# A fused linear-attention and SwiGLU kernel: the last group's outputs over three queues, and one more Strassen pair in group 3

## The chip, the cores and the metric

The kernel runs on one core of a Trainium2 chip. The time is the device time of one execution in microseconds (us); three runs before the change gave 297.36, 297.43 and 297.45, so the median is 297.43. The profile is of one further execution, whose own time was 297.82 us.

## The reference

The inputs are q, k and v with 8 batches, 8 heads, 576 positions and 64 channels, and three weight matrices. What is computed, cut to its core:

```python
q_p, k_p = phi(q), phi(k)                       # phi(x) = elu(x) + 1
kv = einsum('bhsd,bhse->bhde', k_p, v)
num = einsum('bhsd,bhde->bhse', q_p, kv)
den = einsum('bhsd,bhd->bhs', q_p, sum(k_p, axis=2))[..., None] + 1e-06
x = (num / den).transpose(0, 2, 1, 3).reshape(4608, 512)
g, val = x @ w_gate, x @ w_val                  # 512 -> 1536
out = (g * sigmoid(g) * val) @ w_out            # 1536 -> 512, float32
```

## The kernel before

The 4608 tokens are cut into 72 units of 64 (9 per batch), and 8 units make one of 9 groups of 512 tokens. For each group TensorE makes the normalized attention output (`x_prd`), then layer 1 (gate and value), then layer 2 (`l2_prd`), and the results go from SBUF to DRAM. The attention of later batches is prepared between: `phis` (feature map of k and q), `kv_prd` (the 64x64 state of a batch), `chain` and `norm` (denominator, reciprocal, and the scaling of q, `s3_scale`), and `tr`, a transposing DMA on SyncE's queue that turns scaled q for `x_prd`.

**Layer 1.** A column block of 128 hidden features costs 16 matmuls of 512 columns for two blocks of the plain form (`c_chunk`, L826: two matmuls an operation). A *pair* of blocks can be made in Strassen's form instead (`pair_prd`, L351: seven products of four matmuls with 256 columns). A pair needs more work on the other engines: five ScalarE copies or silus (L365, L368) and four VectorE operations (L371 twice, L855, L864), where the two plain blocks need two silus and two multiplications (L374). `NP` says how many of a group's six pairs are made so: 3 in groups 2 and 3, 5 in groups 4 and 5, 6 from group 6 on. With fewer than four pairs, `layer_1` alternates pair products and plain chunks; with four or more it runs the pair products staggered and puts the plain chunks at the end, and fills the first slots with what the group before left over (`tail`).

**Layer 2** is Strassen's form throughout (`prd`, L456): seven products numbered 1 to 7, each for two token tiles `tt` 0 and 1, of six matmuls with 256 columns. The string `ORDER[g]` gives their order: `60` is product 6 of tile 0; a letter after it takes part of its six matmuls (`a`: the first four, `c` the fifth, `d` the sixth, `e` the first five). `M` is the next group's `x_prd`, `J` a `kv_prd`; what stands behind `|` is left to the next group's layer 1. Sums of the hidden tile, `hs` (`h_sum`, L425), feed products 3, 5, 6, 7. A product is taken out of PSUM by `keep` (ScalarE, L465, to a partial sum), `fin` (VectorE, L470, product plus partial sum to the output tile `osb`) or `copy_half` (ScalarE, L461).

**Order.** Every operation of groups 1 to 8 is put on a list with the tiles it reads and writes, and a list of 1362 numbers, `steps`, gives the order in which they are issued. Each engine works strictly in that order.

**Output of the last group (8).** Each quarter of an output tile (128 partitions by 256 columns) goes out in two transfers of 64 rows by 1 KB, `put_1` (L1014), issued by `out_op`. Of 16 transfers, 13 are issued on SyncE's queue (SP), two on ScalarE's and one on GpSimd's (POOL).

**Scaling of q.** `S3[b]`/`SCALE[b]` give the position chunks of batch b that are summed and scaled one group before their batch is first used; `S3L[b]`/`SCALEL[b]` those left to the next group. Batch 4 is done whole: summed as (0,5),(5,9), scaled in threes. Batch 5 is split: (0,5) early, (5,9) late.

`WL` says before which group the weight sums for Strassen's products (`wl_sum`) of the second half of the hidden features are put on the list.

Of the kernel before, what the change touches and what calls it, by code (L numbers as in the profile page):

```python
# [10 lines left out]
ALU = mybir.AluOpType  # L11
AX = mybir.AxisListType

P = 128
# [3 lines left out]
def kernel(  # L18
# [420 lines left out]
    def prd(g, n, tt, fs, seeded):  # L439
# [15 lines left out]
        for (i, f) in enumerate(fs):  # L455
            nc.tensor.matmul(out=(z if n in (2, 3, 5) else x)[:, 0:HD], lhsT=left(f), rhs=right(f),  # L456
                             start=(i == 0 and fs[0] == 0 and (n in (1, 5) or n == 2 and not seeded)),
                             stop=(i == len(fs) - 1), skip_group_check=True)
# [9 lines left out]
    def fin(tt, th, ch, i, from_x):  # L468
        (x, z) = l2_banks(tt)
        nc.vector.scalar_tensor_tensor(out=osb[2 * th + tt][:, HD * ch:HD * ch + HD],  # L470
                                       in0=(x if from_x else z)[:, 0:HD], scalar=1.0 / SC, in1=part[:, 2 * i + tt, :],
                                       op0=ALU.mult, op1=ALU.add)
# [333 lines left out]
    def nm(t):  # L806
        return bank[id(t)]
# [10 lines left out]
    NP = {1: 0, 2: 3, 3: 3, 4: 5, 5: 5, 6: 6, 7: 6, 8: 6}  # L818
# [103 lines left out]
    KVB = {**{b: ["X2", "V2"] for b in range(B)}, 2: ["X0", "X1"], 7: ["X1", "V0"], 6: ["X1", "V0"], 5: ["X1", "V0"]}  # L922
# [34 lines left out]
    def l2_prd(g, n, tt, fs=tuple(range(HF)), done=True):  # L957
# [11 lines left out]
        if n == 1:  # L969
            if sd:  # L970
                op("ACT", 0.3, lambda: copy_half(x, seed_bank(tt)[:, 0:HD], 1.0), [nm(x)], [nm(seed_bank(tt))])
            else:
                op("ACT", 0.3, lambda: keep(tt, 0, True), [nm(x)], [f"part0{tt}"])
        if n == 2:
            if sd:
                op("ACT", 0.3, lambda: copy_half(dst, o1[:, 0:HD], 1.0 / SC), [nm(dst)], [f"o{tt}.0"])
            else:
                op("DVE", 0.34, lambda: fin(tt, 0, 0, 0, False), [nm(z), f"part0{tt}"], [f"o{tt}.0"])
# [6 lines left out]
        if n == 7:  # L985
            op("DVE", 0.34, lambda: fin(tt, 1, 1, 2, True), [nm(x), f"part2{tt}"], [f"o{2 + tt}.1"])
            if last:
                out_op(g, tt, 1, 1, (nc.sync, nc.scalar) if tt else (nc.sync, nc.sync))
        if n == 3:
            op("DVE", 0.34, lambda: fin(tt, 0, 1, 1, False), [nm(z), f"part1{tt}"], [f"o{tt}.1"])  # L990
            if last:
                out_op(g, tt, 0, 1, (nc.sync, nc.gpsimd) if tt else (nc.sync, nc.sync))
            else:
                op("SP", 0.12, lambda: put(g, tt, 0), [f"o{tt}.0", f"o{tt}.1"], [])
        if n == 4:
            if last and tt:
                op("DVE", 0.34, lambda: nc.vector.tensor_scalar(out=o2[:, 0:HD], in0=x[:, 0:HD], scalar1=1.0 / SC, scalar2=None,
                                                                op0=ALU.mult), [nm(x)], [f"o{2 + tt}.0"])
                out_op(g, tt, 1, 0, (nc.sync, nc.scalar))
# [7 lines left out]
    def out_op(g, tt, th, ch, engs=(nc.sync, nc.sync)):  # L1007
        for e in range(2):
            eng = {id(nc.sync): "SP", id(nc.scalar): "ACT", id(nc.gpsimd): "POOL"}[id(engs[e])]
            op(eng, 0.06, lambda e=e: put_1(g, tt, th, ch, e, engs[e]), [f"o{2 * th + tt}.{ch}"], [])  # L1010
# [78 lines left out]
    WL = {2: [(1, 1, 1), (2, 0, 1)], 3: [(2, 1, 1), (3, 0, 1)], 4: [(3, 1, 1)]}  # L1089
# [45 lines left out]
    ORDER[99] = ""; S3[7], SCALE[7], S3L[7], SCALEL[7] = ((0, 1),), ((0, 1),), ((1, 5), (5, 9)), ((1, 3), (3, 6), (6, 9)); S3[6], SCALE[6], S3L[6], SCALEL[6] = ((0, 2),), ((0, 2),), ((2, 5), (5, 9)), ((2, 5), (5, 9),); S3[5], SCALE[5], S3L[5], SCALEL[5] = ((0, 5),), ((0, 3), (3, 5)), ((5, 9),), ((5, 9),)  # L1135

    ORDER.update({g: "10 11 20 21 60 61 50 51 70 71 M 30 31 | 41 40 J" for g in (3,4)})

    def program():
# [21 lines left out]
        0 1 4 14 15 9 17 18 10 5 20 21 23 6 24 26 27 16 29 3 19 30 32 8 2 33 35 36 7 22 38 28 41 25 39 40 42 31  # L1161
        34 44 45 43 37 47 63 46 48 64 49 105 66 12 50 67 69 106 65 70 51 11 72 68 73 52 75 71 13 76 114 78 77 79
        74 81 80 82 84 53 83 85 54 87 86 88 90 55 89 91 107 93 56 94 92 96 95 57 97 99 98 100 58 102 59 101 103
        113 127 104 60 129 108 128 109 131 117 171 133 110 132 130 135 112 115 137 134 139 111 136 125 138 120
        141 116 143 119 142 145 140 118 122 147 146 144 150 124 126 148 153 121 162 151 156 61 165 155 154 123
        168 62 149 152 163 167 158 176 164 157 172 177 169 159 179 166 170 178 160 181 161 197 180 342 199 182
        200 343 183 198 202 184 204 201 206 203 174 207 185 209 208 205 211 186 210 214 215 173 212 218 220 219
        213 222 175 221 187 223 225 216 224 227 217 229 228 188 230 285 226 232 231 189 234 236 235 237 233 240
        242 238 241 245 243 246 239 248 190 247 250 244 249 252 251 253 276 255 191 254 257 256 259 277 192 258
        193 260 262 261 264 194 267 265 268 263 271 266 273 269 272 274 270 284 298 275 300 278 280 299 302 279  # L1170
        301 286 281 304 303 282 306 288 308 305 287 310 307 296 309 289 312 283 314 313 311 316 290 291 318 317
        315 293 321 319 324 322 297 292 333 326 336 294 325 334 195 339 327 328 347 329 196 320 348 504 323 340
        335 338 350 330 341 337 349 331 352 368 332 353 370 354 369 371 355 373 372 375 356 295 377 357 378 380
        379 376 382 381 358 385 386 351 383 389 344 387 391 393 390 392 394 374 384 396 359 398 397 388 400 360
        399 401 395 403 456 405 402 404 407 345 408 406 411 409 413 346 412 361 416 410 414 417 419 415 418 421
        364 423 422 424 420 426 425 362 428 430 429 447 431 363 365 448 427 433 432 435 438 436 439 434 442 437
        444 440 443 445 441 455 469 446 471 449 470 450 473 457 451 475 452 474 472 477 459 476 479 453 478 481
        467 480 454 462 483 458 485 484 460 487 482 464 486 489 488 498 461 491 501 490 366 468 492 505 499 493
        367 507 494 500 506 496 510 508 495 512 466 502 463 515 503 509 517 497 513 465 516 523 514 518 525 519
        511 527 529 524 528 540 526 542 541 545 543 531 547 546 629 550 530 552 548 551 554 532 553 556 544 558  # L1180
        555 561 557 559 563 562 549 566 560 564 568 567 570 565 569 533 572 571 574 573 577 620 579 575 578 582
        580 576 584 534 586 583 588 585 587 590 589 593 581 591 595 594 598 621 521 600 596 602 601 603 599 535
        606 592 604 608 607 611 597 605 612 609 520 614 613 615 536 617 616 522 618 628 610 642 537 619 644 622
        643 624 646 632 623 648 625 626 645 650 635 647 652 649 627 654 651 653 637 656 633 658 634 657 660 655
        700 630 662 661 671 659 663 640 631 674 664 672 641 666 667 677 665 675 679 636 678 682 668 680 684 639
        669 670 687 638 689 688 701 694 538 685 691 696 690 702 683 539 698 673 676 681 686 706 695 703 715 697
        699 717 716 704 720 707 722 721 725 718 708 705 727 726 723 729 728 731 709 719 733 730 736 732 734 738
        737 724 741 739 743 742 745 710 804 744 747 735 749 746 752 748 750 754 753 740 757 755 751 759 758 761
        711 756 763 760 762 765 764 768 712 770 766 769 773 713 693 775 771 777 714 778 767 776 781 774 779 783
        782 772 786 780 784 787 692 789 797 788 790 792 798 791 793 785 803 815 795 794 817 796 816 819 799 807  # L1190
        800 821 820 801 818 823 805 825 822 802 827 824 826 810 829 808 831 871 830 806 833 828 812 832 835 834
        844 872 836 809 847 837 845 838 873 850 846 839 852 840 848 851 855 841 849 853 842 857 814 843 854 860
        874 862 811 861 865 858 875 864 867 813 859 863 856 869 876 882 866 891 870 868 893 892 877 896 894 884
        898 897 901 880 883 903 902 905 895 899 907 904 909 906 908 900 912 910 914 913 917 885 911 915 919 918
        921 886 916 923 920 887 922 925 924 928 878 930 929 933 926 879 881 935 934 931 937 936 888 939 927 938
        941 944 940 889 932 946 890 945 942 949 951 947 950 953 979 952 955 954 943 957 960 980 956 962 948 961
        958 965 968 963 959 969 966 971 972 970 967 974 964 973 975 977 978 981 976 989 990 991 992 993 983 996
        982 998 1000 997 1002 984 1004 999 985 1011 994 1003 1006 1001 1013 988 995 1015 987 1014 1007 1017 1012
        1016 986 1005 1019 1047 1018 1021 1008 1020 1023 1009 1022 1026 1024 1028 1010 1027 1025 1048 1031 1029
        1033 1049 1032 1030 1036 1034 1050 1038 1037 1035 1051 1041 1039 1052 1043 1042 1040 1045 1053 1044 1060  # L1200
# [46 lines left out]
```

## Time and profile before

| | us |
|---|---|
| median of three runs | 297.43 |
| profiled execution, its own time | 297.82 |
| its span, first to last instruction | 296.0 |
| PE busy | 286.4 (97%) |
| weight load (PEld) busy | 212.9 (72%) |
| VectorE (DVE) busy | 258.6 (87%) |
| ScalarE (ACT) busy | 236.3 (80%) |
| GpSimd (POOL) busy | 42.5 (14%) |

Two kinds of view are used. A *timeline* has, for each piece of an engine's work, start and length in us, engine, line, operation, destination and source, and the number of instructions merged into it. A *windows* row has the length of a stretch and then the busy time of PE, PEld, DVE, ACT and POOL, each with its number of instructions, the granted share of TensorE's clock (1.00 nearly everywhere here), the DMA engines' mean busy share and GB/s. Issues of transfers on SP's and ACT's queues appear as SPq and ACTq.

### The profile page before, as it was taken

Reading aid. Unit: us, or ns where it says so; the run is one execution under the profiler, and the core shown is the slowest. Engines: PE = TensorE matmul, PEld = TensorE weight load, DVE = VectorE, ACT = ScalarE, POOL = GpSimd, SP = SyncE. Lnnn points to the kernel's source line nnn. Section 1 sums busy time; section 2 is a strip of 40 time slices with the busy share of each in tenths; the row PEclk is TensorE's granted clock in tenths of the full one; section 3 lists DMA queues with packets and bytes.
Section 4 is the critical chain, followed back from the end, with each engine's and each line's share of the span. In section 5 each row is a group of like instructions: output and inputs, shape, how many; then the busy total and the mean of one; then the engine's idle time right before and its main releaser. Section 6 shows DMA issues by size and latency. Waiting matters only on the chain.

```text
span 296.0 us, 7377 instructions
## 1 busy us (share of the span) xinstructions
PE 286.4 (97%) x2939; PEld 212.9 (72%) x2939; DVE 258.6 (87%) x521; ACT 236.3 (80%) x405; POOL 42.5 (14%) x55
## 2 busy tenths in 40 slices
PE   7899999999999999999999999999999999999991
PEld 5644454454866687668887888788888888788881
DVE  4667889999999998999899999999999999757961
ACT  4773977983998689969999999999986688668830
POOL 8554436500000011000100010000000000000000
PEclk9999999999999999999999999999999999999999
DMA  7999999995598319661960669304140443050014
GB/s 203 193 196 200 205 207 207 196 216 87 81 171 190 64 15 171 162 105 33 147 181 2 105 98 222 61 2 100 44 73 2 99 95 22 2 129 15 0 41 103
DMA packets 41506, 32.92 MB, mean 111 GB/s; under 512 B 16432, under 2 KB 36848, under 8 KB 41472
## 3 DMA queue, kind: packets, MB, share of 16 engines
q0 software_dynamic: 20176, 18.35, 40.7%
q1 hardware_dynamic: 21136, 13.97, 21.0%
q8 instruction: 23, 0.38, 0.5%
q10 hardware_dynamic: 160, 0.13, 0.2%
q14 instruction: 11, 0.09, 0.1%
HBM read 37.75 MB, written 9.44 MB: 159 GB/s over the span
## 4 chain that ended last, share of the span: by engine, by line
issue 50%; PE 43%; DMA 2%; ACT 2%; POOL 1%; POOLq 0%
PE pV L826 7%; PE pX L456 6%; PE pG L826 6%; PE pX L351 5%; PE pX L297 3%; PE pV L297 3%; DMA q<-in_q_dram 2%; PE pG L383 2%; PE pV L383 2%; PE pG L297 2%; PE pV L456 2%; PE pX L826 1%; PE pX L268 1%; PE pV L351 1%; PE pX L187 1%
## 5 line engine op out<-in xcount | busy, mean ns | idle before, releaser
L351 PEld LDWEIGHTS <-wl 128*128 128x128 f16 x414 | 40.3, 98 | 9.6 <-issue 0.2
L456 PEld LDWEIGHTS <-hs 128*128 128x128 f16 x384 | 37.2, 98 | 5.4 <-issue 0.7
L456 PEld LDWEIGHTS <-hT 128*128 128x128 f16 x288 | 27.7, 98 | 5.1 <-DVE hs L425 0.4
L351 PEld LDWEIGHTS <-wg 128*128 128x128 f16 x272 | 26.4, 98 | 5.7
L456 PE MATMUL pX<-ws,hs 128*128 128x256 f16 x240 | 28.8, 273 | 0.1
L826 PE MATMUL pV<-xt,wv 128*128 128x512 f16 x104 | 28.3, 379 | 0.0
L368 ACT ACTIVATE ek<-eq 128x512 f16<-128x512 f32 x34 | 21.3, 625 | 5.3 <-DVE eq L855 5.2
L351 PE MATMUL pV<-xt,wg 128*128 128x256 f16 x168 | 23.9, 273 | 0.0
L826 PE MATMUL pG<-xt,wg 128*128 128x512 f16 x80 | 22.5, 379 | 0.0
L368 ACT ACTIVATE ek<-pV 128x512 f16<-128x512 f32 x34 | 20.3, 597 | 2.7 <-PE pV L351 1.9
L351 PE MATMUL pX<-xs,wl 128*128 128x256 f16 x132 | 19.8, 273 | 0.0
L465 ACT ACTIVATE part<-pX 128x256 f32<-128x256 f32 x40 | 14.3, 386 | 6.4 <-PE pX L456 6.3
L456 PE MATMUL pX<-wo,hT 128*128 128x256 f16 x144 | 19.0, 273 | 0.0
L371 DVE SCALAR_TENSOR_TENSOR r<-pG,rr 128x512 f16<-128x512 f32 x20 | 13.7, 687 | 5.5 <-PE pG L351 5.2
L374 DVE SCALAR_TENSOR_TENSOR hT<-pV,sil 128x512 f16<-128x512 f32 x26 | 17.6, 684 | 0.9 <-PE pV L826 0.3
L425 DVE TENSOR_TENSOR hs<-hT 128x512 f16<-128x512 f16 (+3 forms) x35 | 17.8, 514 | 0.0
L365 ACT ACTIVATE rr<-pX 128x512 f32<-128x512 f32 x27 | 15.9, 598 | 2.4 <-PE pX L351 2.3
L470 DVE SCALAR_TENSOR_TENSOR osb<-pX,part 128x256 f32<-128x256 f32 x32 | 12.9, 419 | 5.2 <-ACT part L465 2.9
L1014 POOL DMA_DIRECT2D out_dram<-osb x1 | 0.6, 562 | 116.8 <-DVE osb L470 116.8
L249 DVE TENSOR_TENSOR qp<-qp,rden 128x768 f16<-128x768 f16 (+3 forms) x19 | 17.2, 906 | 0.0
L826 PEld LDWEIGHTS <-wv 128*128 128x128 f16 x112 | 10.9, 98 | 8.5
L124 ACT ACTIVATE ek<-k 128x1152 f16<-128x1152 f16 x14 | 16.1, 1161 | 1.3 <-DMA k<-in_k_dram 1.3
(187 smaller groups left out, 725.2 us busy)
## 6 DMA issues: line engine op xcount, KB each, us to landing
out_dram<-osb SPq DMA_DIRECT2D x64, 128.0 KB, 2.9
k<-in_k_dram POOLq DMA_DIRECT2D x7, 576.0 KB, 7.4
q<-in_q_dram POOLq DMA_DIRECT2D x7, 576.0 KB, 8.9
v<-in_v_dram POOLq DMA_DIRECT2D x7, 576.0 KB, 6.3
wg<-in_moe_w_gate_dram POOLq DMA_DIRECT2D x5, 256.0 KB, 9.2
wv<-in_moe_w_val_dram POOLq DMA_DIRECT2D x5, 256.0 KB, 9.8
wo<-in_moe_w_out_dram POOLq DMA_DIRECT2D x2, 512.0 KB, 15.1
out_dram<-osb SPq DMA_DIRECT2D x13, 64.0 KB, 2.1
```

The source lines that it names most:

```text
L124: nc.scalar.activation(out=e[:, s, :], in_=src[ix(b)][:, s, :], func=AF.Exp, bias=0.0, scale=1.0)
L249: nc.vector.tensor_tensor(out=qv, in0=qv, in1=rden[:, HL * j0:HL * j1].unsqueeze(2).to_broadcast([P, HL * (j1 - j0), D]), op=ALU.mult)
L297: nc.tensor.matmul(out=ps[:, :], lhsT=src[:, i, P * fb:P * fb + P], rhs=xT[i][g % 2][:, :], start=(i == 0), stop=(i == 3))
L351: nc.tensor.matmul(out=dst[:, HN * e:HN * e + HN], lhsT=lhs, rhs=rhs, start=(n in (1, 5) and e == 0 and c == 0), stop=(c == 1), skip_group ...
L365: nc.scalar.activation(out=dst, in_=halves(src), func=AF.Copy, bias=0.0, scale=scale)
L368: nc.scalar.activation(out=dst, in_=src, func=AF.Silu, bias=0.0, scale=1.0)
L371: nc.vector.scalar_tensor_tensor(out=dst, in0=halves(src), scalar=SC, in1=b, op0=ALU.mult, op1=op1)
L374: nc.vector.scalar_tensor_tensor(out=hT[:, fb, :], in0=pv[:, :], scalar=SC, in1=s[:, :], op0=ALU.mult, op1=ALU.mult)
L425: (eng or nc.vector).tensor_tensor(out=o, in0=a, in1=b, op=op)
L456: nc.tensor.matmul(out=(z if n in (2, 3, 5) else x)[:, 0:HD], lhsT=left(f), rhs=right(f), start=(i == 0 and fs[0] == 0 and (n in (1, 5) or ...
L465: nc.scalar.activation(out=part[:, 2 * i + tt, :], in_=(x if from_x else z)[:, 0:HD], func=AF.Copy, bias=0.0, scale=1.0 / SC)
L826: nc.tensor.matmul(out=dst[:, :], lhsT=src[:, i, P * fb:P * fb + P], rhs=xT[i][g % 2][:, :], start=(i == 0), stop=(i == 3))
```

## The change

In the last group all outputs go by a table, one letter for each of the two halves (S for SyncE, A for ScalarE, P for GpSimd). The last quarter is taken out of PSUM by two engines, 64 partitions each. Product 2 gets a bank of its own (`SEED[8] = 2`: it starts an accumulation in `seed_bank` instead of adding to the bank that product 5 uses), and the products are reordered. Group 3 gets four pairs (and so the other branch of `layer_1`), group 2's order now leaves `41 40 J` to group 3, batch 4's second part is normalized one group later, batch 5's is cut into thirds, and batch 4's state goes to other banks. `steps` is a new list (1373 numbers).

```diff
-                             start=(... (n in (1, 5) or n == 2 and not seeded)),
+                             start=(... (n in (1, 5) or n == 2 and seeded is not True)),
...
-    def fin(tt, th, ch, i, from_x):
+    def fin(tt, th, ch, i, from_x, own=False):
         (x, z) = l2_banks(tt)
+        if own:
+            z = seed_bank(tt)
...
-    NP = {1: 0, 2: 3, 3: 3, 4: 5, 5: 5, 6: 6, 7: 6, 8: 6}
+    NP = {1: 0, 2: 3, 3: 4, 4: 5, 5: 5, 6: 6, 7: 6, 8: 6}
...
-    KVB = {**{b: ["X2", "V2"] for b in range(B)}, 2: ["X0", "X1"], 7: ["X1", "V0"], 6: ["X1", "V0"], 5: ["X1", "V0"]}
+    KVB = {..., 5: ["X1", "V0"], 4: ["X1", "V0"]}
...
-                op("DVE", 0.34, lambda: nc.vector.tensor_scalar(out=o2[:, 0:HD], in0=x[:, 0:HD], ...), [nm(x)], [f"o{2 + tt}.0"])
-                out_op(g, tt, 1, 0, (nc.sync, nc.scalar))
+                lo, hi = slice(0, C), slice(C, 2 * C)
+                op("DVE", 0.34, lambda: nc.vector.tensor_scalar(out=o2[lo, 0:HD], in0=x[lo, 0:HD], ...), [nm(x)], [f"o{2 + tt}.0a"])
+                op("ACT", 0.3, lambda: nc.scalar.activation(out=o2[hi, 0:HD], in_=x[hi, 0:HD], ...), [nm(x)], [f"o{2 + tt}.0b"])
+                op("SP", 0.06, lambda: put_1(g, tt, 1, 0, 0, nc.sync), [f"o{2 + tt}.0a"], [])
+                op("ACT", 0.06, lambda: put_1(g, tt, 1, 0, 1, nc.scalar), [f"o{2 + tt}.0b"], [])
...
+    OUTQ = {(0, 0, 0): "SP", (0, 0, 1): "SP", (1, 1, 0): "SP", (0, 1, 0): "SP", (1, 0, 0): "SA", (1, 1, 1): "SA", (0, 1, 1): "SP"}
+    QUEUE = {"S": ("SP", 0.6, nc.sync), "A": ("ACT", 0.5, nc.scalar), "P": ("POOL", 0.6, nc.gpsimd)}
+
+    def out_op(g, tt, th, ch):
+        for (e, x) in enumerate(OUTQ[(th, ch, tt)]):
+            op(QUEUE[x][0], QUEUE[x][1], lambda x=x, e=e: put_1(g, tt, th, ch, e, QUEUE[x][2]), ...)
...
-    WL = {2: [(1, 1, 1), (2, 0, 1)], 3: [(2, 1, 1), (3, 0, 1)], 4: [(3, 1, 1)]}
+    WL = {2: [(1, 1, 1), (2, 0, 1), (2, 1, 1), (3, 0, 1)], 3: [(3, 1, 1)]}
...
-    S3[5], SCALE[5], S3L[5], SCALEL[5] = ((0, 5),), ((0, 3), (3, 5)), ((5, 9),), ((5, 9),)
+    S3[5], SCALE[5], S3L[5], SCALEL[5] = ((0, 3),), ((0, 3),), ((3, 6), (6, 9)), ((3, 6), (6, 9))
+    S3[4], SCALE[4], S3L[4], SCALEL[4] = ((0, 5),), ((0, 3), (3, 5)), ((5, 9),), ((5, 9),)
-    ORDER.update({g: "10 11 20 21 60 61 50 51 70 71 M 30 31 | 41 40 J" for g in (3,4)})
+    ORDER.update({g: "10 11 20 21 60 61 50 51 70 71 M 30 31 | 41 40 J" for g in (2,3,4)})
+    ORDER[8] = "10c 11c 20c 21c 10d 11d 50e 20d 21d 60 61 51e 50d 51d 70 71 30 40 31 41"; SEED[8] = 2
-    # ORDER[8] was "10c 20c 11c 21c 10d 20d 11d 21d 60 61 50 70 30 40 51 71 31 41"
```

In both versions group 2's order before this line was `10 11 20 21 60 61 50 51 70 71 30 31 M 41 J 40`; the last line of the diff shows the old order of group 8, which stands further up in the file and is overwritten.

## The prediction

> **What bounds the kernel now.** I read the busy table, then windows by group, then the timeline of the last 14 us. The busy table gives PE 286.4 of 296.0 us. The windows below are group 3 (its layer 1, its layer 2), group 4 with its layer 2, and group 5.
>
> ```profile
> 115.10:134.80 19.70, 19.70 (x138) 13.15 (x137) 18.55 (x35) 16.60 (x31) 0.74 (x1) 1.00 0.73 143
> 134.80:145.20 10.40, 10.40 (x108) 9.01 (x106) 10.21 (x22) 10.33 (x18) 1.48 (x2) 1.00 0.45 61
> 145.20:174.00 28.80, 28.80 (x327) 23.82 (x325) 26.76 (x52) 28.02 (x50) 2.22 (x3) 1.00 0.48 92
> 174.00:203.00 29.00, 29.00 (x329) 24.02 (x327) 28.49 (x60) 28.18 (x51) 0.00 (x0) 1.00 0.51 97
> ```
>
> PE is busy in all of every row: up to the last product the time is the sum of PE's matmuls. But DVE and ACT stand at 93 to 98% beside it, so there is little room for more of their work. The end is another matter (timeline; the two L456 pieces at the top are around the last group's only gap on PE).
>
> ```profile
> 282.35 0.62 DVE L425 TENSOR_TENSOR hs<-hs,hT 128x512 f16<-128x512 f16 x2
> ...
> 282.76 0.27 PE L456 MATMUL pV<-wo,hT 128*128 128x256 f16 x1
> ...
> 283.17 2.78 PE L456 MATMUL pX<-ws,hs 128*128 128x256 f16 x24
> ...
> 283.80 9.40 SPq L1014 DMA_DIRECT2D out_dram<-osb  x13
> ...
> 289.20 1.81 ACTq L1014 DMA_DIRECT2D out_dram<-osb  x2
> 289.22 0.81 PE L456 MATMUL pX<-ws,hT 128*128 128x256 f16 x6
> ...
> 290.06 0.56 POOL L1014 DMA_DIRECT2D out_dram<-osb  x1 [116.75 <-DVE osb L470]
> 290.07 0.42 DVE L997 TENSOR_SCALAR osb<-pX 128x256 f32<-128x256 f32 x1 [0.31 <-PE pX L456]
> ```
>
> PE ends at 290.03 (call it E), the last quarter is in SBUF at 290.50, and ACT issues its half of it in the piece that begins at 289.20, at 290.53. SP, however, issues without a real pause until 293.20: 13 issues in 9.40 us. The output tile's own view says when the last began and how long a transfer takes from issue to landing:
>
> ```profile
> L1014 SPq DMA_DIRECT2D out_dram<-osb x13: 467/549/1594, 283.8 to 292.7; - x13
> ...
> DMA to landing us min/median/max: 1.9/2.1/3.7
> ```
>
> So SP sends the other half of the last quarter at 292.65 (a narrower timeline has its last two issues as 1.19 us from 292.02), 2.12 us after ACT sent its half. It lands at 294.66, and 1.34 us of closing waits lead to 296.0. **The last 2.1 us are SP's queue of issues**, nothing else.
>
> **Part 1: three queues.** Counting the table's letters, and the last quarter's S and A: SP issues 8, POOL 5, ACT 3. In program order the last on SP are o0.1, o2.0, o1.1 and the half of o3.0. With products at 0.654 us (six matmuls 0.109 apart), 31 ends at E-0.65 and 40 at E-1.31. Taking out of PSUM costs 0.04 + 0.42 on DVE (the row at 290.07), 0.38 on ACT. So o2.0 is ready at E-0.88, o1.1 at E-0.19, the last half at E+0.46. SP's issues (0.55 each, 0.05 between) then stand at E-0.85, E-0.25, and, free at E+0.35, E+0.50 = 290.53. ACT issues o2.0's half at E-0.85, is free before E, takes its 64 partitions (0.38) and issues at E+0.46. What queues behind ACT's issues is only this; no other engine waits for it. The last issue thus moves from 292.65 to 290.53: **-2.12**. Its landing: 2.0 us, as for the last ones before, up to 2.4 for the one that SP issued at 290.44 among ACT's and POOL's. After the change four transfers are issued in the last 0.75 us, as before between 289.85 and 290.53; I add **+0.15**. Halving the last eviction's partitions costs and saves nothing: the row's length is set by 256 columns.
>
> Two rules of the Trainium skill speak against this part. *DMA: Bandwidth & Descriptors*, section "Issuing engines are not separate DMA queues", says that the three issuers feed the same 16 DMA engines and that several of them save only issue time, "usually small relative to the DMA itself". By it the gain is near zero. The rows say otherwise for 64 KB transfers: issue is 0.6 us of a queue, 13 of them 9.40, while the DMA engines were this busy:
>
> ```profile
> 290.00:292.00 2.00, 0.04 (x1) 0.00 (x0) 0.42 (x1) 0.00 (x0) 0.56 (x1) 1.00 0.67 168
> 292.00:294.00 2.00, 0.00 (x0) 0.00 (x0) 0.00 (x0) 0.00 (x0) 0.00 (x0) 1.00 0.51 119
> ```
>
> A third to a half of them is free, so saving issue time is saving the end. I take the row (-1.97), and keep 0 as the rule's end.
>
> *SBUF — State Buffer*, the "DVE blocks DMA" box in its section on the two sides of SBUF, says that a transfer issued by GpSimd gets no descriptors while DVE runs certain two-port operations; the same page puts such a transfer at some 3.1 us instead of 0.62. The one POOL row here, 0.56 long, ran beside DVE's at 290.07, and landed in 2.0 us; eight early loads were issued one behind another, about 0.73 apart. By the row five POOL issues are harmless (the last at about E+0.03, landing E+2.05, before SP's); by the rule they are not (rival 3). I take the row: DVE's fp16 `hs` sums from SBUF to SBUF, the likelier blockers, are done before the first POOL issue at about E-4.0, and only evictions from PSUM follow. The trace also has GpSimd's closing drain, which ends 2.73 us after that one issue, so at about E+2.75, close to SP's last landing at E+2.65: no loss, but no slack.
>
> **Part 2: the new order of products.** PE's gap before 283.17 is 0.31 us (the piece at 282.76 is followed by the next start after 0.41 instead of 0.109). It waits for the L425 sums that end at 282.97. Now `50e`, five matmuls that need only sums of the first five blocks, ready by about 281.7, stand ahead of `60`: 0.545 us of cover for 0.31. **-0.31.** Product 2's own bank costs nothing: `keep` and `fin` are the same instructions at the same lengths, and `51e`, `50d`, `51d` lie between `61` and `70` to hide the 0.38 of `keep` there. If the cover were gone, 0.31 would be back.
>
> **Part 3: a fourth pair in group 3.** PE pieces of the chain of waits price it:
>
> ```profile
> 86.20 0.44 PE pX L351 x4
> 86.64 0.43 PE pV L826 x2
> ```
>
> A pair is 7 x 0.436 = 3.05, two plain blocks 8 x 0.432 = 3.46: **-0.40**, all on the path, since PE has no gaps there. It adds on DVE 3 x 0.69 + 0.41 - 2 x 0.684 = +1.1, on ACT 5 x 0.60 - 2 x 0.60 = +1.8. ACT in group 3 goes from 26.93 (16.60 + 10.33) in 30.1 to 28.7 in 29.7, 97%: what group 4 has (28.02 of 28.8) without a PE gap. Group 3 takes group 4's form of layer 1 and of the order around `M`, so group 4's row is the nearest.
>
> **Part 4: scaling split.** Batch 4's second part (0.68 + 0.42 + 0.68 for the sums, 1.22 for scaling, plus a second reciprocal step of 0.5) leaves group 3's layer 1, about half of it for group 3's end and half for group 4. Thirds for batch 5 cost 3 x (0.55 + 0.35 + 0.54) instead of 0.82 + 0.68 + 0.49 + 0.42 + 0.81 + 0.68: +0.42. Together DVE gets +2.0. Over groups 2 to 5 (84.7 to 203.0, two more rows of the same view with 18.97 and 10.43 for group 2) it is busy 113.4 of 118.3, idle 4.9, so this fits, with 2.5 left after PE's shortening. The transposing DMAs move on SP's queue, but each is issued ten or more PE products before the `x_prd` that reads it, against a landing of 2.9 us; the loads on POOL's queue move by at most a few us and are read a group later. The `WL` and `KVB` edits move no weight sum by more than a few products and cost nothing. Unknown is whether DVE or ACT, this full, now and then holds PE. From below: -0.2 (before, one pair product of group 6 came 0.22 late, at 211.6, behind ACT; a new order may lose that). From above: +2.0, all the added DVE work. Nearest are groups 4 and 5 with the same loads and no gap: I take **+0.2**.
>
> **Sum.** -1.97 - 0.31 - 0.40 + 0.2 = -2.48: span 296.0 to 293.5, the profiled execution 297.82 to 295.3. That execution is 0.39 over the median; I take the same difference off the median, 297.43 to **294.9**.
>
> **Rivals.** (1) *DVE becomes the bound* from group 3 to 6: for it, 98% in group 5; against it, PE without gaps there. Priced in full: -1.97 - 0.31 - 0.40 + 2.0 = -0.68, 296.7; in half, 295.7. (2) *GpSimd is the last to finish*: its drain with five transfers behind it runs 1 us longer than the 2.73: 295.8. Against: they are spread over 4 us. (3) **The slower side**: each POOL transfer occupies GpSimd as long as the drain did, 2.73 us (the skill's 3.1 is near). Five from E-4.0 = 286.0 end at 299.7, and land 1.4 later at 301.1 instead of 294.66; less 0.51 from PE: +5.9, 303.3. It decides from 286.0 + 5s + 1.4 = 294.66 + 0.51, s = 1.55 us each. Against: the 0.73 of the early loads. (4) *The three queues do not help*, since the DMA engines are the limit: -0.51, 296.9. Against: their share of 0.5 to 0.67. That the outputs stay on SP is not possible: the table names the engines.
>
> **Chances.** Forecast 0.65, rivals 0.12, 0.12, 0.06, 0.05. The forecast's own span is 294.2 (-0.2 for the unknown, no contention: 294.4, and 0.2 for the fit of profile to median) to 295.4; up to 296.2 comes rival 2 and half of rival 1, together about 0.8. A measurement of this kernel tells some 0.2%, 0.6 us, from no change. Faster by more than that: forecast, rivals 1 and 2; rival 4 is within it; rival 3 and a rest slower: 0.88, 0.05, 0.07.
>
> **What would show it.** Right: SP 8 issues, the last starting 0.5 us after PE's end; from PE's end to the span's end about 4.0 us instead of 5.97; no gap of 0.3 ahead of product 60; PE rows full in groups 3 to 6, and PE's end near 289.5. Wrong: POOL's L1014 issues longer than 1.5 us or landing after SP's; PE gaps at L351 in groups 3 to 6 that name ACT or DVE; a closing wait that begins at GpSimd.

## The result and the profile after

The changed kernel took 295.73 us (median of four runs, 295.50 to 296.03) against 297.39 for the kernel before, run beside it: a ratio of 0.9946, with a 95% interval of 0.9929 to 0.9964. That is 1.66 us faster where 2.5 were forecast. The profiled execution took 295.81 us, its span is 294.0; before, 297.82 and 296.0.

The same stretches as before the change (windows: length, then busy time of PE, PEld, DVE, ACT, POOL with instruction counts, granted clock, DMA share, GB/s):

```profile
115.10:134.80 19.70, 19.70 (x218) 14.48 (x216) 18.74 (x36) 16.98 (x32) 0.74 (x1) 1.00 0.77 132
134.80:145.20 10.40, 10.40 (x107) 8.98 (x106) 10.19 (x21) 10.32 (x18) 1.48 (x2) 1.00 0.41 63
145.20:174.00 28.80, 28.50 (x321) 23.25 (x319) 27.91 (x58) 27.72 (x50) 1.48 (x2) 1.00 0.65 117
174.00:203.00 29.00, 28.85 (x324) 23.72 (x323) 28.61 (x58) 27.49 (x50) 0.74 (x1) 1.00 0.53 87
```

In group 3 PE is full as foreseen; ScalarE (ACT) stands at 27.30 there (16.98 + 10.32), where 28.7 were forecast. In the two rows behind it PE is no longer full: 0.30 and 0.15 us are missing, although ScalarE is less busy there than before (27.72 and 27.49 after 28.02 and 28.18). Busy time shows only half of what is lost, because the recorded lengths of matmuls overlap: four of them started within 0.436 count as 0.60 busy, so a start that comes 0.31 late leaves a hole of 0.15. The end, as a timeline:

```profile
289.23 2.07 SPq L1022 DMA_DIRECT2D out_dram<-osb  x3
289.24 0.50 ACTq L1022 DMA_DIRECT2D out_dram<-osb  x1
289.28 0.82 PE L456 MATMUL pX<-ws,hT 128*128 128x256 f16 x6
...
290.13 0.42 DVE L1000 TENSOR_SCALAR osb<-pX 64x256 f32<-64x256 f32 x1 [0.23 <-PE pX L456]
290.20 0.53 POOL L1022 DMA_DIRECT2D out_dram<-osb  x1 [0.79 <-DVE osb L472]
290.58 0.38 ACT L1002 ACTIVATE osb<-pX 64x256 f32<-64x256 f32 x1 [1.38 <-DVE osb L1000]
290.99 0.47 ACTq L1022 DMA_DIRECT2D out_dram<-osb  x1
```

and the last group's transfers by queue, from the view of the output tile (shortest, median and longest issue in ns, first and last start):

```profile
L1022 SPq DMA_DIRECT2D out_dram<-osb x8: 466/522/728, 285.9 to 290.8; - x8
L1022 POOL DMA_DIRECT2D out_dram<-osb x5: 527/529/562, 286.1 to 290.2; - x5
L1022 ACTq DMA_DIRECT2D out_dram<-osb x3: 473/498/556, 288.0 to 291.0; - x3
```

PE's last product ends at 290.10 (E again). SP's last issue starts at E+0.65, GpSimd's at E+0.10, ScalarE's at E+0.89, and the span ends at E+3.86, where it was E+6.00. The queue of issues behind PE's end is gone. One thing in the timeline was not foreseen: the two halves of the last eviction do not run side by side. ScalarE's starts when VectorE's has ended, and the view names VectorE's L1000 as what released it.

To see where the rest went, take as a mark the first matmul of each `x_prd` (L268, which multiplies a batch's state by the transposed q); it stands some 4 us ahead of a group's end. Differences of start times in us, with three of the runs told below:

| | before | change | `e2_tail` | `e6_act45` | `e10_mix` |
|---|---|---|---|---|---|
| first mark from the span's start | 81.87 | 81.97 | 81.99 | 81.73 | 81.80 |
| to the mark at 141 (groups 2, 3) | 59.45 | 59.06 | 59.45 | 59.06 | 59.05 |
| to the mark at 171 (group 4) | 29.65 | 29.95 | 29.66 | 30.20 | 29.66 |
| to the mark at 201 (group 5) | 29.62 | 30.36 | 29.66 | 30.10 | 29.62 |
| to the mark at 226 (group 6) | 25.10 | 24.86 | 25.10 | 24.85 | 25.09 |
| to PE's end | 64.35 | 63.90 | 63.90 | 63.90 | 63.90 |
| PE's end to the span's end (the tail) | 6.00 | 3.86 | 3.87 | 3.85 | 4.12 |

The first row differs from run to run (81.48 to 82.26 among runs whose list is the same up to there, and the kernel before lies inside); the others repeat to a few hundredths wherever the code is the same. So the change gained 2.14 at the tail, 0.45 in the last groups and 0.39 in group 3, and lost 0.30 in group 4 and 0.74 in group 5; group 6 gave 0.24 back. (The 2.14 is the difference of two single executions; `e3_middle` below shows how far the tail of before varies.) Three new gaps of PE, 0.31 each, make up 0.93 of the loss of 1.04: the last matmuls ahead of them start near 151.7, 172.9 and 175.3. Another 0.09 is a short wait near 176.8. The first gap, in the timeline of the change:

```profile
150.37 0.63 ACT L368 ACTIVATE ek<-eq 128x512 f16<-128x512 f32 x1
...
150.89 0.60 ACT L368 ACTIVATE ek<-pV 128x512 f16<-128x512 f32 x1
...
151.40 0.60 PE L351 MATMUL pV<-xt,wl 128*128 128x256 f16 x4
151.52 0.58 ACT L365 ACTIVATE pV<-pV 128x512 f32<-128x512 f32 x1
...
152.15 0.60 PE L351 MATMUL pV<-xs,wl 128*128 128x256 f16 x4
```

The four matmuls at 151.40 take 0.436, so the next were due at 151.84. They start at 152.15, just after ScalarE's eviction (L365) of their bank ends at 152.10. That eviction stands behind two activations (L368). The kernel before has the same five pieces in another order:

```profile
150.68 0.58 ACT L368 ACTIVATE ek<-pV 128x512 f16<-128x512 f32 x1
...
151.29 0.58 ACT L365 ACTIVATE pV<-pV 128x512 f32<-128x512 f32 x1
151.66 0.60 PE L351 MATMUL pV<-xt,wl 128*128 128x256 f16 x4
151.79 0.62 ACT L368 ACTIVATE ek<-eq 128x512 f16<-128x512 f32 x1
...
152.10 0.49 PE L351 MATMUL pV<-xs,wl 128*128 128x256 f16 x3
```

There the activation of `eq` comes after the eviction, and PE goes on after 0.44. The other two gaps are alike. At the start of group 5 (timeline of the change):

```profile
172.15 1.08 ACT L284 ACTIVATE xt<-pG 128x512 f16<-128x512 f32 x2
...
173.10 0.62 ACT L284 ACTIVATE xt<-pV 128x512 f16<-128x512 f32 x1
173.28 0.49 PE L351 MATMUL pG<-xt,wg 128*128 128x256 f16 x3 [0.15 <-ACT xt L284]
...
173.74 1.28 ACT L922 ACT_TABLE_LOAD   x1
...
175.04 0.58 ACT L365 ACTIVATE pV<-pG 128x512 f32<-128x512 f32 x1
...
175.67 0.60 PE L351 MATMUL pG<-xs,wl 128*128 128x256 f16 x4
```

and ScalarE's pieces there before the change:

```profile
171.56 1.08 ACT L284 ACTIVATE xt<-pG 128x512 f16<-128x512 f32 x2
172.54 1.09 ACT L284 ACTIVATE xt<-pV 128x512 f16<-128x512 f32 x2
173.55 0.58 ACT L365 ACTIVATE pV<-pG 128x512 f32<-128x512 f32 x1
...
174.55 1.28 ACT L920 ACT_TABLE_LOAD   x1
```

The change copies one of the `pV` blocks first, so that both `pG` copies come some 0.6 later than they did; and it loads ScalarE's table (1.28) ahead of the L365 eviction that PE needs, not behind it.

### The profile page after: what moved, and what is told of

Read it like the earlier page. It is cut to its first block, busy times and chain, and to the rows that moved or that the text cites. A ratio compares the mean times of both kernels' runs of the same rounds, so it can differ in the third digit from the quotient of the medians.

```text
span 294.0 us, 7414 instructions
## 1 busy us (share of the span) xinstructions
PE 286.3 (97%) x2951; PEld 214.3 (73%) x2951; DVE 260.6 (89%) x528; ACT 237.8 (81%) x409; POOL 45.1 (15%) x59
## 4 chain that ended last, share of the span: by engine, by line
PE 90%; ACT 3%; DMA 2%; DVE 2%; issue 1%; POOL 0%; ACTq 0%; POOLq 0%
PE pX L456 18%; PE pV L351 14%; PE pG L351 13%; PE pX L351 7%; PE pV L828 7%; PE pG L828 5%; PE pV L456 5%; PE pX L828 3%; PE pV L297 3%; PE pX L297 3%; DMA q<-in_q_dram 2%; PE pG L383 2%; PE pV L383 2%; PE pG L297 2%; PE pX L187 1%; PE pX L268 1%
## 5 line engine op out<-in xcount | busy, mean ns | idle before, releaser
L351 PEld LDWEIGHTS <-wg 128*128 128x128 f16 x280 | 27.1, 98 | 4.9 <-issue 0.3
L351 PE MATMUL pV<-xt,wg 128*128 128x256 f16 x176 | 25.0, 273 | 0.0
L368 ACT ACTIVATE ek<-eq 128x512 f16<-128x512 f32 x35 | 21.9, 625 | 3.5 <-DVE eq L857 3.3
L368 ACT ACTIVATE ek<-pV 128x512 f16<-128x512 f32 x35 | 20.9, 597 | 3.2 <-PE pV L351 2.6
L828 PE MATMUL pV<-xt,wv 128*128 128x512 f16 x88 | 23.4, 379 | 0.0
L351 PE MATMUL pG<-xs,wl 128*128 128x256 f16 x118 | 19.8, 272 | 0.1
L371 DVE SCALAR_TENSOR_TENSOR r<-pG,rr 128x512 f16<-128x512 f32 x23 | 15.7, 682 | 4.5 <-PE pG L351 3.5
L1022 POOL DMA_DIRECT2D out_dram<-osb x5 | 2.7, 541 | 110.3 <-DVE osb L472 110.3
L456 PE MATMUL pX<-wo,hT 128*128 128x256 f16 x138 | 18.2, 273 | 0.0
L828 PE MATMUL pG<-xt,wg 128*128 128x512 f16 x64 | 17.6, 379 | 0.0
L351 PE MATMUL pV<-xs,wl 128*128 128x256 f16 x114 | 16.7, 273 | 0.1
L371 DVE SCALAR_TENSOR_TENSOR hT<-pG,ek 128x512 f16<-128x512 f32 x23 | 15.7, 684 | 0.8 <-PE pG L351 0.7
```

What stands on the lines that cost most here:

```text
L351: nc.tensor.matmul(out=dst[:, HN * e:HN * e + HN], lhsT=lhs, rhs=rhs, start=(n in (1, 5) and e == 0 and c == 0), stop=(c == 1), skip_group ...
L368: nc.scalar.activation(out=dst, in_=src, func=AF.Silu, bias=0.0, scale=1.0)
L371: nc.vector.scalar_tensor_tensor(out=dst, in0=halves(src), scalar=SC, in1=b, op0=ALU.mult, op1=op1)
L828: nc.tensor.matmul(out=dst[:, :], lhsT=src[:, i, P * fb:P * fb + P], rhs=xT[i][g % 2][:, :], start=(i == 0), stop=(i == 3))
```

## The experiments

Theory A: the loss in the middle is the order of the work on ScalarE's queue, as the new list has it in groups 4 and 5. Rivals: VectorE is the bound (rival 1 of the prediction), or ScalarE is simply full, so that some wait comes in any order. All ratios are to the kernel before, with 95% intervals; its medians beside the three sets of runs were 297.36, 297.12 and 297.39. The ratios are those on record; in the fourth decimal they need not equal the quotient of the medians.

**The parts by themselves.** `e1_queues` is the kernel before with only the engines of the 16 issues as in the table:

```diff
-                out_op(g, tt, 0, 0)
+                out_op(g, tt, 0, 0, (nc.sync, nc.gpsimd))
...
-                out_op(g, tt, 1, 1, (nc.sync, nc.scalar) if tt else (nc.sync, nc.sync))
+                out_op(g, tt, 1, 1, (nc.sync, nc.scalar) if tt else (nc.sync, nc.gpsimd))
...
-                out_op(g, tt, 0, 1, (nc.sync, nc.gpsimd) if tt else (nc.sync, nc.sync))
+                out_op(g, tt, 0, 1, (nc.sync, nc.gpsimd))
...
-                    out_op(g, tt, 1, 0)
+                    out_op(g, tt, 1, 0, (nc.sync, nc.scalar))
```

> The kernel before with only the issuing engines of the last group's 16 transfers changed to the new table (the last quarter stays one eviction on VectorE); order and middle stay. Theory A (SyncE's queue held the end, three queues free it): about 295.4, which is 2.0 below before; PE's end unchanged, from it to the span's end about 4.0 us instead of 5.97. Rival B (the tail gained little and the new middle gave what was gained): within 0.6 of before.

Measured: 296.30 us, ratio 0.9967 (0.9953 to 0.9982), where 295.4 was expected. In the trace the tail is 4.14 instead of 6.00, but PE, whose end was expected to stay, ends 0.27 later. The timeline shows why:

```profile
287.18 0.82 PE L456 MATMUL pV<-ws,hs 128*128 128x256 f16 x6
...
287.79 0.56 ACTq L1014 DMA_DIRECT2D out_dram<-osb  x1
287.84 0.82 PE L456 MATMUL pX<-ws,hs 128*128 128x256 f16 x6
288.40 0.38 ACT L465 ACTIVATE part<-pV 128x256 f32<-128x256 f32 x1 [0.64 <-PE pV L456]
...
288.83 0.81 PE L456 MATMUL pV<-wo,hs 128*128 128x256 f16 x6 [0.18 <-ACT part L465]
```

The product into `pV` is complete at 288.00, and before this edit ScalarE evicted it at 288.03. Now it first spends 0.56 on the issue, evicts at 288.40, and PE's next product into that bank comes 0.34 late. With the old order of products the three queues are thus worth 1.6 in the trace and 1.06 by the medians; the new order has no eviction by ScalarE behind such an issue that PE waits for.

`e2_tail` is the kernel before with all that the change does to the last group (queues, halves, order and bank of product 2), and `e3_middle` is the change with the last group of before:

```diff
-    ORDER[8] = "10c 20c 11c 21c 10d 20d 11d 21d 60 61 50 70 30 40 51 71 31 41"
+    ORDER[8] = "10c 11c 20c 21c 10d 11d 50e 20d 21d 60 61 51e 50d 51d 70 71 30 40 31 41"; SEED[8] = 2
```

> The kernel before up to the last group's layer 2, from there the change's own code and order. Theory A (the tail gained 2.0 to 2.1 by the queues and 0.31 by the new order of products, and the new middle lost 0.3 to 0.4): 295.0, faster than the change itself by some 0.4 to 0.7, with the 0.31 gap ahead of product 60 gone and the 0.22 one in group 6 still there. Rival B (the middle's fourth pair gained its 0.40): slower than the change, about 296.1.

> The change up to the last group's layer 2, from there the kernel before. Theory A: the middle alone is no gain, 0.40 less for the pair, 0.93 more for three waits of PE for ScalarE in groups 4 and 5, 0.22 less in group 6: before plus 0.3, about 297.7. Rival B: before minus 0.4, about 297.0.

Measured: `e2_tail` 295.24 us, 0.9929 (0.9912 to 0.9946); `e3_middle` 297.54, 0.9999 (0.9988 to 1.0009). So the last group is the whole gain. The middle alone brings nothing: it has the three gaps (0.309, 0.314, 0.311 at 151.75, 172.88 and 175.27), which cost what the fourth pair and group 6 give. Its trace has one thing more. The last group is that of before, yet the tail is 5.20, not 6.00 (view of the output tile):

```profile
L1014 SPq DMA_DIRECT2D out_dram<-osb x13: 466/553/1047, 284.3 to 292.6; - x13
```

The longest of SP's 13 issues took 1.05 here and 1.59 before, so the last starts at E+2.05 and not at E+2.62; the other 0.23 lies behind that start. The same tail thus differs by 0.8 between these two executions, and a gain read from one pair of traces is uncertain by as much.

**VectorE or ScalarE, load or order.** `e12_dve` is the change with VectorE's denominators of batches 4 and 5 cut to one block in each chunk, `e13_act` the change with ScalarE's exponentials of k and its copies of v cut for batches 5 to 7:

```diff
-            op("DVE", 0.07 + 0.147 * n, lambda c=c: s3_prod(b, c), ...)
+            op("DVE", 0.07 + 0.147 * n, lambda c=c, w=((j0, j0 + 1) if b in (4, 5) else c): s3_prod(b, w), ...)
...
-        nc.scalar.activation(out=e[:, s, :], in_=src[ix(b)][:, s, :], func=AF.Exp, bias=0.0, scale=1.0)
+        n = 64 if e is ek and b in (5, 6, 7) else J * D
+        nc.scalar.activation(out=e[:, s, 0:n], in_=src[ix(b)][:, s, 0:n], func=AF.Exp, bias=0.0, scale=1.0)
```

> The change, with VectorE's products, sums and reductions for the denominators of batches 4 and 5 cut to one of the blocks in each chunk (the other denominators are left out); order unchanged, some 3.5 us less work of VectorE. Rival 1 of the prediction (VectorE is the bound): the three gaps of PE go, 294.8. Theory A (ScalarE's order): the three gaps stay, 295.6 to 295.7.

> The change, with ScalarE's exponentials of k cut to 64 of 576 columns and its copies of v to one block of nine for batches 5 to 7 (the rest is left out); order unchanged, some 4 us less work of ScalarE in each of groups 3 to 5. Theory A in its wide form (ScalarE's queue is behind, because it is full): all three gaps go, 294.8. In its narrow form (what stands directly ahead of the wanted instruction): the gap near 151.7 (two activations ahead of it) and that near 175.3 (the table's load ahead of it) stay, only the one near 172.9 goes: 295.4.

Measured: 295.38 (0.9934, 0.9918 to 0.9950) and 295.41 (0.9934, 0.9917 to 0.9951), neither told apart from the change; `e12_dve` lies between the times that the two sides named, so the gaps decide. The change has in the same windows of groups 4 and 5

```profile
144.90:174.00 29.10, 28.80 (x324) 23.52 (x322) 28.21 (x58) 28.02 (x50) 1.48 (x2) 1.00 0.65 118
```

beside its row from 174.00 above; `e12_dve` has

```profile
144.90:174.00 29.10, 28.80 (x323) 23.53 (x322) 26.35 (x58) 28.04 (x49) 1.48 (x2) 1.00 0.65 119
174.00:203.00 29.00, 28.85 (x326) 23.73 (x325) 28.48 (x59) 27.57 (x50) 0.74 (x1) 1.00 0.50 88
```

and `e13_act`:

```profile
144.90:174.00 29.10, 28.80 (x324) 23.52 (x322) 28.21 (x58) 25.29 (x50) 1.48 (x2) 1.00 0.67 119
174.00:203.00 29.00, 28.85 (x324) 23.71 (x323) 28.61 (x58) 24.59 (x50) 0.74 (x1) 1.00 0.51 80
```

VectorE has up to 1.9 us less to do (28.21 to 26.35), ScalarE 2.7 and 2.9 less, and PE misses the same 0.30 and 0.15. The three gaps are 0.308, 0.314 and 0.311 in the one, 0.310, 0.314 and 0.309 in the other. So neither engine's amount of work makes them. Rival 1 falls, and so does "ScalarE is full"; only the short wait near 176.8 is gone in `e12_dve` (group 5 takes 30.27 instead of 30.36). That 295.4 was named for `e13_act` and came is luck, since no gap went. My narrow expectation for the gap near 172.9 was set on a wrong instruction: the exponential that stands ahead of those copies is one of q, which `e13_act` does not cut.

**The order on ScalarE.** `e5_act5` is the change with two of ScalarE's instructions moved in the list, 669 (a copy into `xt`) and 642 (the table's load), both in group 5. `e6_act45` also moves 547 (the activation of `eq`) and, with it, 552 (a VectorE product) in group 4:

```diff
-        ... 662 674 669 706 677 666 675 707 667 676 678 ...
+        ... 662 674 706 677 666 675 707 667 669 676 678 ...
-        ... 642 708 682 671 685 673 687 681 672 709 683 690 ...
+        ... 708 682 671 685 673 687 681 672 709 683 642 690 ...
...
-        ... 551 547 557 538 554 559 552 556 558 561 ...
+        ... 551 557 538 554 559 556 547 558 552 561 ...
```

> The change, with two of ScalarE's instructions moved later in group 5 only: one copy of a plain block behind two copies of a pair, and the loading of ScalarE's table behind an eviction. Theory A (the order on ScalarE's queue makes the waits in the middle): PE's gaps near 172.9 and 175.3 are gone, the one near 151.7 stays, 0.62 us less than the change: 295.1. Rival B (ScalarE or VectorE is simply full there, so that the wait only moves): a gap of the same size appears later in group 5 or 6 and the time stays at 295.7.

> As the one before, and in group 4 one activation of ScalarE is moved behind the eviction that its neighbour products wait for. Theory A: the gap near 151.7 goes too, 0.93 us less than the change: 294.8, and PE's end 0.9 us earlier than in the change. Rival B: 295.4 to 295.7, with gaps elsewhere in groups 4 to 6.

Measured: 295.48 (0.9938, 0.9925 to 0.9952) and 295.52 (0.9945, 0.9932 to 0.9957). Each gap that was aimed at is gone, as theory A has it; each time others come, as rival B has it, and the 295.1 and 294.8 that theory A named were missed. In `e5_act5` five smaller ones open between 177 and 189, together 0.51, the largest 0.18 near 181.9, and group 5 takes 30.10 instead of 30.36, where 29.74 was expected. In `e6_act45` these stay, and a larger one opens in group 4 (timeline):

```profile
153.44 0.63 ACT L368 ACTIVATE ek<-eq 128x512 f16<-128x512 f32 x1 [0.58 <-DVE eq L857]
...
153.97 0.58 ACT L368 ACTIVATE ek<-pV 128x512 f16<-128x512 f32 x1
...
154.58 0.58 ACT L365 ACTIVATE pV<-pG 128x512 f32<-128x512 f32 x1
...
155.22 0.27 PE L351 MATMUL pG<-xs,wl 128*128 128x256 f16 x1 [0.39 <-ACT pV L365]
```

It is the same pattern one pair later: an activation of `eq`, now waiting 0.58 for VectorE's sum, stands ahead of the eviction that frees PE's bank. PE misses 0.55, more than the 0.31 that was mended. The moves show that the order makes the gaps come and go; they do not give a good order.

**An order known to be good.** `e10_mix` keeps the change up to the end of group 3 and in the last group, and takes the order of groups 4 to 7, and batch 5's chunks, from the kernel before:

```diff
-    S3[5], SCALE[5], S3L[5], SCALEL[5] = ((0, 3),), ((0, 3),), ((3, 6), (6, 9)), ((3, 6), (6, 9))
+    S3[5], SCALE[5], S3L[5], SCALEL[5] = ((0, 5),), ((0, 3), (3, 5)), ((5, 9),), ((5, 9),)
```

> The change up to the end of group 3 (fourth pair, batch 4's scaling split) and its last group, with the order of groups 4 to 7 and batch 5's scaling of the kernel before. Theory A (PE's new waits lie in how the order of groups 4 and 5 was written for batch 5's thirds, the fourth pair does not bring them): no PE gap in groups 4 and 5, 0.4 us less than the kernel with the change's last group alone: 294.8. Rival B (a fourth pair and the second part of batch 4's scaling fill ScalarE and VectorE so that some wait comes in any order): gaps of together 0.4 to 0.9 us in groups 4 and 5, 295.3 or more.

Measured: 294.95 us, 0.9917 (0.9899 to 0.9936). Its windows of groups 4 and 5:

```profile
145.20:174.00 28.80, 28.80 (x326) 23.81 (x325) 28.26 (x56) 27.99 (x51) 2.22 (x3) 1.00 0.60 109
174.00:203.00 29.00, 29.00 (x329) 24.00 (x328) 28.49 (x60) 28.15 (x51) 0.00 (x0) 1.00 0.49 94
```

ScalarE has more to do than in the change, VectorE about as much, and PE has no gap. So the fourth pair and the second part of batch 4's scaling fit, and what cost time is the new order of groups 4 and 5, written around batch 5's thirds. Order and thirds went back together here; that the order is what matters rests on the moves above, and whether the thirds can be had without gaps is left open. The tail is 0.26 longer than in the change (4.12): VectorE begins one of its last evictions 0.36 later against PE's end, though the order there is the same, and SP's last issue starts at E+0.90 instead of E+0.65. What holds that eviction was not looked into.

**The tail.** `e4_half` lets ScalarE write its half of the last quarter to another tile, `e7_best` (on top of `e6_act45`) lets VectorE take out all 128 partitions and SP and ScalarE issue the halves, `e9_two` is the change without GpSimd's queue:

```diff
-                op("ACT", 0.3, lambda: nc.scalar.activation(out=o2[hi, 0:HD], in_=x[hi, 0:HD], ...))
+                op("ACT", 0.3, lambda: nc.scalar.activation(out=part[hi, 0, :], in_=x[hi, 0:HD], ...))
...
-                op("DVE", 0.34, lambda: nc.vector.tensor_scalar(out=o2[lo, 0:HD], in0=x[lo, 0:HD], ...))
-                op("ACT", 0.3, lambda: nc.scalar.activation(out=o2[hi, 0:HD], in_=x[hi, 0:HD], ...))
+                op("DVE", 0.34, lambda: nc.vector.tensor_scalar(out=o2[:, 0:HD], in0=x[:, 0:HD], ...))
...
-    OUTQ = {(0, 0, 0): "SP", (0, 0, 1): "SP", (1, 1, 0): "SP", (0, 1, 0): "SP", (1, 0, 0): "SA", (1, 1, 1): "SA", (0, 1, 1): "SP"}
+    OUTQ = {(0, 0, 0): "SA", (0, 0, 1): "SA", (1, 1, 0): "SA", (0, 1, 0): "SA", (1, 0, 0): "SA", (1, 1, 1): "SA", (0, 1, 1): "SA"}
```

> The change, with ScalarE's half of the last quarter written to another tile (a free slot of the partial sums) and sent from there. Theory A (ScalarE's half eviction began only after VectorE's because both write one tile): it begins beside VectorE's at 0.04 after PE's end instead of 0.49, ScalarE's last issue comes 0.45 earlier, and the time falls by 0.2 to 0.45, to about 295.4. Rival C (the two wait for one another because both read one PSUM bank, or SyncE's issue ends last anyway): no change, 295.7.

> As the one before, and VectorE takes all 128 partitions of the last quarter out of PSUM, as before the change; SP and ScalarE issue a half each. Theory A (ScalarE's half of the eviction, waiting behind VectorE's, is what makes the last transfer 0.4 us later than foreseen): ScalarE's last issue starts 0.5 instead of 0.9 us after PE's end, and the end is 0.2 us earlier, SP's last issue being the next in time: 294.6. Rival D (GpSimd's closing drain, which ends 3.0 us after PE's end, is as late as the last landing): the end does not move, 294.8.

> The change with its last group's transfers on two queues, SP and ScalarE, eight each, none on GpSimd. Theory A (what ScalarE issues stands ahead of evictions that free banks for PE, as in the run with the queues alone): one or more PE gaps of 0.3 us in the last 5 us, evictions late: 296.2. Rival D (GpSimd's closing drain is what the end waits for, so that its absence is a gain): no PE gap, end 3.5 instead of 3.9 us after PE's end: 295.4.

Measured: `e4_half` 295.74 us (0.9944, 0.9928 to 0.9960): ScalarE's half still starts 0.45 after VectorE's (290.56 and 290.11), released by it, so the shared output tile is not the cause, and the time is rival C's. What the two still share is the PSUM tile that they read; that it is the reason was not tried by itself. `e7_best` 295.52 (0.9943, 0.9930 to 0.9955), the same as `e6_act45`: ScalarE's last issue starts at E+0.49 as expected, but the tail shrinks by 0.07 only, 3.85 to 3.78. GpSimd's closing drain ends at E+3.01 in both, while the last landing moves from E+2.95 to E+2.80: this is what rival D expected, though nothing else was run to confirm it. `e9_two` 296.13 (0.9968, 0.9955 to 0.9980): PE has no new gap, so the 296.2 of theory A came without the gaps that it named; the tail is 5.11. ScalarE's part of its timeline:

```profile
289.42 0.38 ACT L461 ACTIVATE osb<-pX 128x256 f32<-128x256 f32 x1 [2.73 <-DMA out_dram<-osb]
...
289.83 1.38 ACTq L1022 DMA_DIRECT2D out_dram<-osb  x2
291.31 0.38 ACT L1002 ACTIVATE osb<-pX 64x256 f32<-64x256 f32 x1 [1.51 <-issue]
291.72 0.47 ACTq L1022 DMA_DIRECT2D out_dram<-osb  x1
```

Eight issues on ScalarE's queue hold its own evictions: its half of the last quarter waits for issues until 291.31, 1.69 after PE's end (289.62), where it was 0.49. With GpSimd's five issues on the other two queues the tail is thus 1.25 longer than in the change; GpSimd has no evictions to hold up. Other splits over SP and ScalarE, with fewer on ScalarE, were not tried.

`e11_best` joins what helped: `e10_mix`, the whole last quarter on VectorE, and in group 6 one activation behind the eviction it stood ahead of:

```diff
-        ... 907 910 900 904 912 909 914 ...
+        ... 907 910 904 912 909 900 914 ...
```

> As the one before, VectorE takes the whole last quarter out of PSUM, and in group 6 one activation of ScalarE is moved behind the eviction that PE waits for near 211.5. Theory A: that gap of 0.22 us goes, the tail gives 0.1, 0.3 less than the one before: 294.5. Rival B (in a full group the wait only moves): only the tail's 0.1.

Measured: 294.75 us, 0.9911 (0.9892 to 0.9930), the fastest here, 0.2 under `e10_mix` where theory A had 0.3. The intervals overlap, but each of its four runs (294.67 to 294.82) is below each of the other's (294.83 to 295.02). Its tail is 3.94 instead of 4.12; the gap of 0.21 at 211 is gone and one of 0.13 at 214 has come, rival B's pattern again.

## Why the prediction was right, and where a size was off

**Part 1 (−1.97)** measured −2.14 at the tail between the two traces, and −1.33 against the tail of `e3_middle` (5.20), whose last group is that of before. By the medians `e2_tail` gained 2.12 with parts 1 and 2, and part 2 is 0.45 in the traces, so my estimate for part 1 is about −1.7. The place was right: SP issues 8, the last 0.65 after PE's end (0.50 forecast), since its issue before took 0.73 instead of 0.55. The half that ScalarE takes was forecast to be issued at E+0.46 and was at E+0.89, because it waited for VectorE's. That cost little: its landing, E+2.95, is 0.30 after the E+2.65 that I had for the last, but from the last landing to the span's end it took 0.91 instead of the 1.34 that I carried over. The sentence "no other engine waits for it" held for the new order only; with the old one (`e1_queues`) PE waits 0.34. Of the two rules, *DMA: Bandwidth & Descriptors* is borne out in that several issuers saved issue time only, but that time was not small here: 1.3 to 2.1 us of the end. The box in *SBUF — State Buffer* was not put to the test: GpSimd's five issues took 0.53 to 0.56 each and landed in 2.0 to 2.8 us, but, as I had counted on, VectorE's last `hs` sum ended at 285.19, ahead of the first of them at 286.15, and only evictions from PSUM ran beside them. Rival 3 falls by these lengths, rival 4 by the tail. Of rival 2 the cost was wrong, since the drain with five transfers ends 2.91 after the last issue's start, 0.2 later than with one (2.70) and not 1 us; but it ends 0.06 after the last landing, so GpSimd is about as late as the transfers.

**Part 2 (−0.31)** measured −0.45. The gap ahead of product 60 is gone, and so are two of 0.08 that I had overlooked: in the kernel before, two starts in the last group (286.52 and 289.22) come 0.188 after the ones ahead of them instead of 0.109, in the change none does. That the gain is larger than forecast is luck.

**Part 3 (−0.40)** measured −0.39, and −0.40 again in `e10_mix` against `e2_tail` (59.05 and 59.45).

**Part 4 (+0.2)** is the step that was mis-sized: groups 4 to 6 measured +0.30 + 0.74 − 0.24 = **+0.80**. I priced it by busy shares ("Nearest are groups 4 and 5 with the same loads and no gap") and by VectorE's added work as the upper end. The runs put another thing in its place: the gaps come from what stands directly ahead of an eviction on ScalarE's queue, keep their size when either engine has much less to do, and were to be had from the diff, whose list is rewritten in groups 4 and 5 as well. One part of the lower end came true: the wait at 211 is gone, and group 6 is 0.24 shorter.

**The sum.** With the start (+0.10, not of the change) these make −2.08 in the trace, where −2.48 was forecast. A second term was off by nearly as much: I took the profiled execution to lie 0.39 above the median after the change, as before it; it lies 0.08 above. A likely reason, which no run settles, is the long tail of the one execution profiled before: in `e3_middle`, with a tail of 5.20, profiled time and median agree (297.53 and 297.54). So 295.73 stands where 294.9 was forecast: inside the range of 294.2 to 296.2, but above 295.4, where the forecast's own part of it ended. The room that took it in was kept for rivals 1 and 2, neither of which came true, so that the number fell inside is in part luck. Rival 1, priced in half, gives 295.7 too, and is wrong all the same: VectorE was not what PE waited for.

## What to carry to other kernels

Where several engines are full, their busy shares do not say whether a new order will make PE wait: walk the list of the engine that frees PE's banks and ask of each eviction what stands directly ahead of it (an activation 0.6, a table's load 1.28, an issue 0.5). A transfer's issue is work of the engine that issues it, so give the last outputs first to queues whose engine has no evictions left. And mend a wait by going back to an order that is known to run full rather than by moving single instructions, which here made new waits each time. Where a queue of issues sets the end, read that end in more than one execution before pricing it.

## What the runs showed of the hardware

An issue of a 64 KB output took 0.47 to 0.73 us in the change, whichever the queue, and on ScalarE's it held up that engine's next eviction. GpSimd's closing drain ended 2.91 us after the start of its last issue in the change, and 3.02 to 3.05 in `e1_queues`, `e10_mix` and `e11_best`, with five transfers each; with one it was 2.70 before and 2.80 in `e3_middle`. So four transfers more cost it 0.1 to 0.35. An eviction of 64 partitions by 256 columns took as long as one of 128 partitions (0.42 on VectorE, 0.38 on ScalarE). In the change VectorE and ScalarE took their halves of one PSUM tile one after the other (0.42 + 0.03 + 0.38), the second released by the first, so splitting that eviction saved nothing; whether they could have run side by side was not tried.
